# Attention over 512 heads on one core: the output tile gets ten buffers, and each store is issued later

## The chip, the cores and the metric

The kernel runs on 1 core of one Trainium2 chip. The metric is the device time of one execution in microseconds (us). Before the change the median of 4 runs is 816.46 us (815.45 to 819.59).

## The reference

```python
B, H, Sq, Sk, D = 16, 32, 192, 1024, 128
scores = jnp.einsum("bhqd,bhkd->bhqk", q, k) * scale   # scale = D ** -0.5
p = _softmax(scores, axis=-1)
return jnp.einsum("bhqk,bhkd->bhqd", p, v)
```

All tensors are bf16. For each of the 512 heads, 192 queries look at 1024 keys of width 128, and the softmax-weighted sum of 1024 values of width 128 comes out. Per head, K and V are 256 KB each, Q and the output 48 KB each.

## The kernel before

**Units.** Four heads make a quad; there are NQ = 128 quads, numbered x. A quad's scores are 8 key tiles x 192 queries = 1536 columns for each of the four heads, cut into three blocks of 512 columns, so there are NF = 384 blocks, f = 3x + b. The output work of a quad is cut into three pieces, s = 3x + i.

**The way of a quad.** SyncE (SP) loads V, K and Q of a quad (L552, L543, L530) into one of five buffers each (`f_vs`, `f_kn`, `f_qn`). VectorE (DVE) transposes K in 32x32 blocks (`turn_k`, L740) and Q (`turn_q`, L752). GpSimd (POOL) puts K into the order the matmuls want (`order`, L601) and copies V beside a column of ones (`spread`, L612); it does these in one fixed order: a block of K, the two halves of V of the quad before, two more blocks of K. TensorE (PE) makes the scores of a block (`qk`, L639), the four heads in four 32-row groups. ScalarE (ACT) takes the exponential of a block in two instructions, one head (L838) and three heads (L841). PE multiplies the exponentials with V and the ones (`pv`, L662), four blocks behind the scores (LAG = 4), so that a row's sum stands beside its result. DVE divides by the sum and writes the output tile `f_ob` (`onorm`, L761: a reciprocal, L768, and a multiplication, L772).

**What waits for what.** A load of V(x) waits until `pv` has done piece 3(x-5)+1, a load of K(x) until the K transposes of quad x-5 are done, a load of Q(x) for nothing of its own. SP's order in the loop is V(n+3), K(n+5), Q(n+5) for n = 0 to 127. PE takes a block's scores only after POOL's `order` of that block and after ACT's L838 of the block before. At the end DVE checks that all row sums lie in a safe range; a flag `redo` is then read by every engine (L21), and a second, general path is run if it is set. It isn't set with these inputs.

**The stores.** Two quads (GQ = 2) share one buffer of `f_ob` and are stored by one DMA of 384 KB; the list `stores` has 63 such pairs and two single quads of 192 KB at the end, 65 stores. Store i writes from buffer i % NSO and adds 16 to the semaphore of that buffer. DVE's first `onorm` of store i waits until store i - NSO has landed (L770). A store waits (L522) until DVE has come past its last piece. ACT issues a store behind block f = 3(x+c)+6, where x+c is the quad after the pair, that is six blocks behind the last block of the pair. 62 stores have such an f below NF. The other three (one pair, two single quads) are issued by SP at the very end of its list (L584). The function `stored` (L586) waits for all buffers' semaphores; SP runs it last.

The stores issued by ACT go through another DMA queue (q10 in the profile) than SP's loads (q1).

Of the kernel before, what the change touches and what calls it, by code (L numbers as in the profile page):

```python
# [15 lines left out]
def _only_if(nc, redo, hints):  # L16
    def wrap(body):
        def run(eng):
            name = "redo_%d" % nc.next_id()
            with eng.register() as r:  # L20
                eng.reg_load(r, redo[0:1, 0:1])  # L21
                eng.br_ne(r, 0, on_true=name + "_do", on_false=name + "_end").branch_hint(hints[eng.engine])
                with nc.body(name + "_do", valid_engines=[eng.engine]):
                    body(eng)
                    eng.br(name + "_end")
                nc.switch_bb(name + "_end")
        return run
    return wrap


def _general_path(nc, q, k, v, out, redo, hints, stored, G=16, NS=2, LAGS=(2, 4, 5, 7), ROUTES=(R_W, R_W, R_EA)):
# [16 lines left out]
    NPT = L_PV - L_EV + 2  # L48
    NSO = 2
    NRS = 4  # L50
# [6 lines left out]
    def route(u):  # L57
        return ROUTES[u % len(ROUTES)]
# [19 lines left out]
    with ExitStack() as es:  # L78
        def sb(name, shape, dt):
            return es.enter_context(nc.sbuf_tensor(name, shape, dt))  # L80
# [4 lines left out]
        def sem(name):  # L85
            return es.enter_context(nc.semaphore(name))
# [3 lines left out]
        vs = sb("vs", [128, NS, G, KT_TILES, 128], BF16)  # L90
        ob = sb("ob", [128, NSO, PPG, 4, 128], BF16)
        ss = sb("ss", [128, NSS, SK], F32)
# [13 lines left out]
        svl = [sem("svl%d" % i) for i in range(NS)]  # L106
        sst = [sem("sst%d" % i) for i in range(NSO)]
        s_qk = sem("s_qk")
# [24 lines left out]
        def store_cnt(g):  # L133
            return 48 * (g // NSO + 1)

# [12 lines left out]
        @_only_if(nc, redo, hints)  # L148
        def sync_general(e):
            stored(e)  # L150

            def loads(g):
                s = g % NS
                last_u = (g - NS + 1) * UPG - 1
                h0 = g * G
                if g >= NS:
                    e.wait_ge(s_qk, last_u + 1)
                e.dma_start_transpose(
                    kt[:, s], kf[h0:h0 + G].rearrange("g k d -> (g k) d")
                ).then_inc(sxk[s], 16)  # L160
                e.dma_start_transpose(
                    qt[:, s], qf[h0:h0 + G].rearrange("g k d -> (g k) d")
                ).then_inc(sxq[s], 16)
                if g >= NS:
                    e.wait_ge(s_pv, last_u + 1)
                e.dma_start(
                    vs[:, s], vf[h0:h0 + G].rearrange("g (p t) d -> p g t d", t=KT_TILES)
                ).then_inc(svl[s], 16)

            def stores(g):  # L170
                so = g % NSO
                e.wait_ge(s_on, (g + 1) * PPG)
                h0 = g * G
                og = of[h0:h0 + G]
                e.dma_start(
                    og[:, 0:128, :].rearrange("h p d -> p h d"),
                    ob[:, so].rearrange("p pg (x y) d -> p (pg x) (y d)", y=2)[:, :, 0:128],
                ).then_inc(sst[so], 16)
                oab = og[:, 128:192, :].rearrange("(pg x) p d -> x p pg d", x=2)
                e.dma_start(oab[0], ob[0:64, so, :, 1, :]).then_inc(sst[so], 16)  # L180
                e.dma_start(oab[1], ob[64:128, so, :, 1, :]).then_inc(sst[so], 16)

            for g in range(min(NS, NGR)):
                loads(g)
            for g in range(NGR):
                if g + NS < NGR:
                    loads(g + NS)
                stores(g)
            for so in range(min(NSO, NGR)):
                n_uses = len(range(so, NGR, NSO))  # L190
                e.wait_ge(sst[so], 48 * n_uses)

        @block.sync
        def _(e):
            sync_general(e)
            stored(e)

        @block.gpsimd
        @_only_if(nc, redo, hints)
        def _(gp):  # L200
            gp.memset(ones[:], 1.0).then_inc(s_setup, 1)
            gp.wait_ge(s_setup, 1)
            gp.affine_select(
                ident[:], ones[:], [[1, 128]], ALU.is_equal, 0.0, base=0, channel_multiplier=-1
            ).then_inc(s_setup, 1)

            def shift(u):
                gp.wait_ge(s_max, u + 1)
                if u >= NX:
                    gp.wait_ge(s_tr, u - NX + 1)  # L210
                gp.tensor_tensor(
                    x_sb[:, u % NX, :], ss[:, u % NSS, :],
                    nb[:, u % NSS: u % NSS + 1].to_broadcast([128, SK]), ALU.subtract,
                ).then_inc(s_xp, 1)

            for u in range(NU):
                if route(u) == R_W:
                    shift(u)
# [202 lines left out]
def _attention_kernel(nc, q, k, v, out):  # L421
# [9 lines left out]
    NF = 3 * NQ  # L431
# [5 lines left out]
    AHEAD = 3  # L437
    NKN, NVS, NKT, NVP = 5, 5, 2, 2
    GQ = 2
    NSO = 3  # L440
    VB = 136

    qf = q.rearrange("b h s d -> (b h) s d")
# [4 lines left out]
    stores = [(x, GQ) for x in range(0, NQ - GQ, GQ)] + [(NQ - 2, 1), (NQ - 1, 1)]  # L448
    EARLY = NF - 9

    with ExitStack() as outer:
# [28 lines left out]
        with ExitStack() as es:  # L480
# [44 lines left out]
                ).then_inc(s_st[so], 16)  # L525


            store_at = {3 * (x + c) + 6: i for i, (x, c) in enumerate(stores) if 3 * (x + c) + 6 < NF}

            def load_q(e, x):  # L530
                e.dma_start(
# [54 lines left out]
            def stored(e):  # L586
                for so in range(NSO):
                    e.wait_ge(s_st[so], 16 * len(range(so, len(stores), NSO)))
# [259 lines left out]
def bass_standalone__mha_softmax__near_ridge_kernel(  # L848
    nc: bass.Bass,
    q: bass.AP,  # L850
    k: bass.AP,
    v: bass.AP,
    out: bass.AP,
):
    _attention_kernel(nc, q, k, v, out)
# [28 lines left out]
```

## Time and profile before

| | |
|---|---|
| median of 4 runs | 816.46 us |
| the profiled execution, its own time | 818.72 us |
| its span, first to last instruction | 817.0 us |
| outside the span | 1.72 us |
| ACT L838, one of 384 | 597 ns |
| ACT L841, one of 384 | 1445 ns |
| DVE transposes of K, idle before them for the landing of K | 62.0 us of 66.3 |
| POOL copies of V, idle before them for the landing of V | 209.0 us of 213.5 |
| PE busy, by the modelled ends of its matmuls | 98% |
| granted TensorE clock, mean | 0.998 |

How to read it: the span is what the profiler saw from the first to the last instruction. An engine's busy share is a mean over the whole run, and a busy engine need not be the one that sets the pace. Idle time "before" an instruction is time in which its engine did nothing, and the profile names what ended it.

### The profile page before, as it was taken

How to read it: one execution, taken by the hardware profiler on the slowest of the kernel's cores; microseconds unless marked ns; L12 is line 12 of the kernel's file. 1: busy time of each engine (PE TensorE's matmuls, PEld its weight loads, DVE VectorE, ACT ScalarE, POOL GpSimd, SP SyncE). 2: the span in 40 equal slices, each digit the busy share in tenths (PEclk: the TensorE clock that was granted, in tenths of full speed). 3: DMA queues.
4: the chain of work that ended last, by engine and by line, in shares of the span. 5: the costliest groups of instructions: out<-in, count | busy, mean ns of one | idle time of the engine just before them, and what ended most of it. 6: DMA issues, size and time to landing. Idle time of an engine off the chain costs nothing. (4 is left out here: it accounts for less than half of the span.)

```text
span 817.0 us, 71454 instructions
## 1 busy us (share of the span) xinstructions
PE 801.9 (98%) x32996; PEld 715.0 (88%) x32996; DVE 604.3 (74%) x1293; ACT 750.0 (92%) x772; POOL 551.0 (67%) x648
## 2 busy tenths in 40 slices
PE   8999999999999999999999999999999999999997
PEld 6888888888888888888888888888888888888886
DVE  4677777777777777777777777777777777777775
ACT  6899999999999999999999999999999999999995
POOL 5667667667766766766676676676766766766674
PEclk9999999999999999999999999999999999999999
DMA  7999999999999999999999999999999999999992
GB/s 265 401 405 405 409 405 405 409 404 406 408 403 406 408 403 407 407 404 408 408 402 409 407 404 403 398 406 399 398 407 398 398 407 397 380 405 395 392 379 68
DMA packets 138454, 319.16 MB, mean 391 GB/s; under 512 B 7216, under 2 KB 56368, under 8 KB 122160
## 3 DMA queue, kind: packets, MB, share of 16 engines
q1 hardware_dynamic: 105536, 294.22, 91.9%
q10 hardware_dynamic: 32880, 24.58, 9.0%
q14 instruction: 32, 0.26, 0.1%
q8 instruction: 6, 0.10, 0.0%
HBM read 293.60 MB, written 25.17 MB: 390 GB/s over the span
## 5 line engine op out<-in xcount | busy, mean ns | idle before, releaser
L841 ACT ACTIVATE f_pt<-f_s 128x1536 bf16<-128x1536 f32 x384 | 554.9, 1445 | 0.1
L654 PE MATMUL f_s<-f_qt,f_kt 32*128 32x192 bf16 (+1 forms) x20528 | 422.7, 226 | 8.4 <-PEq L637 7.6
L683 PE MATMUL f_o<-f_vp,f_pt 128*64 128x129 bf16 x12368 | 425.9, 222 | 1.9 <-PEq L637 1.5
L683 PEld LDWEIGHTS f_o<-f_vp,f_pt 128*64 128x64 bf16 x12368 | 363.0, 110 | 51.1 <-issue 24.9
L616 POOL COPY f_vp<-f_vs 128x1024 uint32<-128x1024 uint32 x256 | 259.7, 1043 | 213.5 <-DMA f_vs<-in_v_dram 209.0
L654 PEld LDWEIGHTS f_s<-f_qt,f_kt 32*128 32x128 bf16 x20528 | 349.0, 92 | 45.6 <-issue 11.6
L747 DVE STREAM_TRANSPOSE f_kx<-f_kn 128x768 uint32<-128x768 uint32 (+1 forms) x384 | 335.1, 873 | 66.3 <-DMA f_kn<-in_k_dram 62.0
L607 POOL COPY f_kt<-f_kx 128x768 uint32<-128x768 uint32 (+1 forms) x384 | 294.6, 786 | 41.9 <-DVE f_kx L747 38.0
L838 ACT ACTIVATE f_pt<-f_s 128x512 bf16<-128x512 f32 x384 | 229.3, 597 | 58.6 <-PE f_s L654 17.9
L772 DVE TENSOR_TENSOR f_ob<-f_o,f_rinv 128x256 bf16<-128x256 f32 x381 | 161.7, 424 | 13.3 <-DVE f_rinv L768 0.3
L768 DVE RECIPROCAL f_rinv<-f_o 128x2 f32<-128x2 f32 x381 | 63.3, 166 | 128.1 <-PE f_o L683 126.2
L756 DVE STREAM_TRANSPOSE f_qt<-f_qn 128x384 uint32<-128x384 uint32 x128 | 73.0, 571 | 0.0
L825 ACT ACTIVATE f_pt<-f_ones 128x1536 f32<-128x1536 bf16 x3 | 4.2, 1472 | 0.0
L595 POOL MEMSET f_vp<- 128x1088 uint32 (+1 forms) x3 | 3.8, 1310 | 0.0
L683 PE MATMUL f_s<-f_vp,f_pt 128*64 128x129 bf16 x96 | 3.2, 220 | 0.0
L683 PEld LDWEIGHTS f_s<-f_vp,f_pt 128*64 128x64 bf16 x96 | 2.9, 110 | 0.2
L825 ACT ACT_TABLE_LOAD x1 | 1.3, 1283 | 1.2 <-PEq L869 1.2
L696 PE MATMUL f_o<-f_ones 128*128 128x512 bf16 x2 | 1.0, 620 | 1.1 <-POOL f_ones L592 1.1
L720 DVE MEMSET f_pt<- 128x256 uint32 x4 | 1.1, 272 | 0.9 <-PEq L869 0.9
L713 PE MATMUL f_o<-f_bad,f_ones 128*1 128x1 bf16 x1 | 0.2, 164 | 1.3 <-DVEq L814 1.3
L772 DVE TENSOR_TENSOR f_ob<-f_s,f_rinv 128x256 bf16<-128x256 f32 x3 | 1.3, 425 | 0.1
L768 DVE RECIPROCAL f_rinv<-f_s 128x2 f32<-128x2 f32 x3 | 0.5, 171 | 1.1 <-PE f_s L683 1.1
(15 smaller groups left out, 5.7 us busy)
## 6 DMA issues: line engine op xcount, KB each, us to landing
f_kn<-in_k_dram SPq DMA_DIRECT2D x127, 1024.0 KB, 18.1
f_vs<-in_v_dram SPq DMA_DIRECT2D x127, 1024.0 KB, 16.3
f_qn<-in_q_dram SPq DMA_DIRECT2D x127, 192.0 KB, 14.2
out_dram<-f_ob ACTq DMA_DIRECT2D x62, 384.0 KB, 9.5
f_vs<-in_v_dram SPq DMA_DIRECT2D x2, 512.0 KB, 6.5
f_kn<-in_k_dram SPq DMA_DIRECT2D x2, 512.0 KB, 4.5
out_dram<-f_ob SPq DMA_DIRECT2D x1, 384.0 KB, 3.5
out_dram<-f_ob SPq DMA_DIRECT2D x2, 192.0 KB, 2.0
```

The lines of the kernel that those rows point to most:

```text
L595: return gp.memset(part.bitcast(U32), 0x3F803F80)
L607: gp.tensor_copy(kt[:, x % NKT].bitcast(U32).rearrange("p U (j s u) c -> p U j s (u c)", s=2, u=2)[:, lo:hi], kx[:, x % 2].rearrange("p (U ...
L616: gp.tensor_copy(vp[:, x % NVP, 2 * T * i: 2 * T * i + 2 * T, 0:D].bitcast(U32), vs[:, x % NVS, 2 * i: 2 * i + 2, :].rearrange("p a (t d) ...
L654: ins = pe.matmul(S[:, c0: c0 + n1 - n0], kt[r, x % NKT, 2 * t + h, :, c], qt[r, x % R, h, n0:n1, c], start=w == 0 and g == 0, stop=w == 3 ...
L683: ins = pe.matmul(O[64 * z: 64 * z + 64, u, 0:129], pt[:, x % R, 2 * y + z, t * SQ + 64 * j: t * SQ + 64 * j + 64], vp[:, x % NVP, (2 * y ...
L747: dve.transpose(kx[:, x % 2].rearrange("p (U s j u) -> p s u U j", s=2, j=32, u=2)[:, :, :, lo:hi], kn[:, x % NKN].rearrange("p (s u U i) ...
L756: dve.transpose(qt[:, x % R].bitcast(U32).rearrange("p b (y j u) c -> p u y b (j c)", y=3, u=2), qn[:, x % NKN].rearrange("p (u y b i) -> ...
L768: dve.reciprocal(ri, O[:, :, 128]).then_inc(s_rc, 1)
L772: dve.tensor_tensor(ob[:, so, 6 * a + 2 * w: 6 * a + 2 * w + 2, :], O[:, :, 0:128], ri.unsqueeze(2).to_broadcast([128, 2, D]), ALU.mult,). ...
L825: return act.activation(part.bitcast(F32), ones[:, 0:1].to_broadcast([128, 2 * T * SQ // 2]), ACT_FN.Copy)
L838: act.activation(pt[:, x % R, 0, c], s1_ps[:], ACT_FN.Exp, scale=scale).then_inc(s_e1, 1)
L841: act.activation(pt[:, x % R, 1:4, c], s3_ps[f % 2][:], ACT_FN.Exp, scale=scale).then_inc(s_e3, 1)
```

## The change

The output tile has ten buffers in place of three (`f_ob` and its semaphores). Each store's block is 42 blocks (seven pairs of quads, HOLD = 7) later than it was, and ACT issues only the stores for which that block is at most NF - 12 = 372. That leaves 54 stores on ACT in place of 62; the first is issued behind block 54 in place of 12, the last behind block 372. The other 11 (nine pairs and the two single quads; ten pairs' worth of bytes) are issued by SP behind its last load, in the same last loop as before. A buffer is written again 20 quads later in place of 6, so the distance from a store's issue to the next write of its buffer is about eleven blocks before and after. The general path's GpSimd body also waits for all stores first; that body isn't run.

```diff
         def _(gp):
+            stored(gp)
             gp.memset(ones[:], 1.0).then_inc(s_setup, 1)
...
-    NSO = 3
+
+    NSO, HOLD = 10, 7
...
-            store_at = {3 * (x + c) + 6: i for i, (x, c) in enumerate(stores) if 3 * (x + c) + 6 < NF}
+            store_at = {3 * (x + c) + 6 + 6 * HOLD: i for i, (x, c) in enumerate(stores)
+                        if 3 * (x + c) + 6 + 6 * HOLD <= NF - 12}
```

## The prediction

> **What bounds the kernel now.** I read the page first. Three things stand near their limit: PE, ACT and the DMA.
>
> ```profile
> span 817.0 us, 71454 instructions
> ...
> PE 801.9 (98%) x32996; PEld 715.0 (88%) x32996; DVE 604.3 (74%) x1293; ACT 750.0 (92%) x772; POOL 551.0 (67%) x648
> ...
> DMA  7999999999999999999999999999999999999992
> GB/s 265 401 405 405 409 405 405 409 404 406 408 403 406 408 403 407 407 404 408 408 402 409 407 404 403 398 406 399 398 407 398 398 407 397 380 405 395 392 379 68
> ...
> q1 hardware_dynamic: 105536, 294.22, 91.9%
> q10 hardware_dynamic: 32880, 24.58, 9.0%
> q14 instruction: 32, 0.26, 0.1%
> ```
>
> The transfers are full from the second slice to the last but one, and fall from about 405 GB/s to 380-395 late. PE's ends are modelled, so its 98% doesn't decide. ACT does two instructions per block, 597 + 1445 ns. To see its pace without disturbance I took the groups of ACT in the window 60 to 110 us, then ACT's waits from 110 to 800 us.
>
> ```profile
> L838 ACT ACTIVATE f_pt<-f_s 128x512 bf16<-128x512 f32 x25 | 14.9, 597 | 2.9
> ```
>
> ```profile
> POOL f_vp L616 <- DMA f_vs<-in_v_dram: 186.4, 109, 3.0
> DVE f_rinv L768 <- PE f_o L683: 103.3, 256, 0.5
> DVE f_kx L747 <- DMA f_kn<-in_k_dram: 50.0, 89, 1.5
> POOL f_kt L607 <- DVE f_kx L747: 25.5, 84, 1.2
> PEld f_o L683 <- issue: 19.6, 116, 0.5
> ACT f_pt L838 <- PE f_s L654: 10.2, 26, 0.9
> ```
>
> In the quiet window ACT idles 2.9 / 25 = 0.116 us a block and waits for nobody: its L838 rows start 2.05 us apart there (151.05, 153.10, 155.16 in another quiet stretch), two instructions that overlap a little and that gap, and ACT sets the pace. From 110 us on it has 26 longer gaps, 10.2 us. Without the 0.116 that every block has, 10.2 - 26 x 0.116 = **7.2 us are lost to late scores**. Behind them stand POOL, which waits for V in 109 places, and DVE, which waits for K in 89. At the gap of 0.87 us before 686.3 us, POOL's copy of V at 681.99 had waited 3.03 us for its landing, the next blocks of K stood behind it on POOL, and PE idled 0.69 us before 685.12. So the kernel is ACT-paced, with a transfer stream that is just too slow for it and falls 7.2 us behind in 690 us.
>
> Are the loads late for want of bandwidth, or of free buffers? SP's own rows answer:
>
> ```profile
> 683.48 0.59 SPq L555 DMA_DIRECT2D f_vs<-in_v_dram  x1
> 684.11 1.09 SPq L546 DMA_DIRECT2D f_kn<-in_k_dram  x1
> 685.25 5.62 SPq L531 DMA_DIRECT2D f_qn<-in_q_dram  x1
> ```
>
> The Q load waits for no semaphore, and its issue still took 5.62 us: the queue was full. The waits of SP's loads that the profile puts down to PE and DVE are of this kind too: V(107) was issued at 665.0 us, and the reciprocal behind the `pv` that frees its buffer ran at 657.78. So free buffers stand idle for some 7 us before their load gets into the queue. Bandwidth is short.
>
> The tail shows how it is short. Windows of 785 to 795 and 799.6 to 802.8 us (after the times: PE, PEld, DVE, ACT, POOL, clock, DMA share, GB/s):
>
> ```profile
> 785.00:795.00 10.00, 10.00 (x430) 8.90 (x427) 8.02 (x18) 9.43 (x11) 6.26 (x9) 1.00 1.04 400
> 799.60:802.80 3.20, 2.56 (x100) 2.17 (x99) 2.64 (x5) 3.09 (x4) 2.56 (x3) 1.00 0.07 25
> ```
>
> 405 / 16 is 25.3 GB/s: at the end as much as one of sixteen DMA engines is still working, some 7 us behind the others, and the last load (V of quad 127, landed 803.2 us) waits for it. An engine that gets extra work holds up every load. Instruction fetches (q14) are such work if they go to one engine: from 110 to 800 us they are 26 packets, 0.21 MB, at 25.3 GB/s 8.3 us, about the 7.2 lost. That they all go to one engine is my inference. **The skill** against this: "Runtime: NRT & Kernel Launch", section "Instruction fetch mechanics", calls the cost of refilling mostly hidden. By that rule the 7.2 us would be ordinary shortage; the sum below is the same by either, since it takes the loss from ACT's gaps.
>
> **The change, part by part.**
>
> *Stores held for seven pairs.* From block 12 to block 54 no store runs. Seven stores fewer stand before every later load. One store takes 393,216 B / 405 GB/s = 0.97 us by bytes, or 9.0% of 817.0 / 62 = 1.19 us by its queue's share. Seven are 6.8 to 8.3 us by which each load lands earlier; I take 6.8, the end on measured bytes. Can so much be stored up? Buffers that now idle about 7 us take it, and behind them the queue is deep (16.3 us from V's issue to its landing), so no DMA engine runs dry when SP must wait for a buffer. The lead isn't spent later: seven stores stay outstanding up to the end.
>
> *What it is worth.* ACT cannot go below 2.05 us a block, so the gain is the smaller of lead and loss: min(6.8, 7.2) = **6.8 us**. The startup gaps (7.0 us of idle in 5 places before 40 us) come before any store and stay, and so does the gap of 0.82 us before 803.88, where DVE is held up by the 1.04 us check (L784) ahead of the last Q transpose. What is late next is ACT itself.
>
> *ACT's issues.* Eight fewer at 0.38 us. They are issued while L841 runs (785.10 lies before its row at 785.20, with no gap): worth 0.
>
> *DVE's wait for a buffer.* Store i is issued behind block 6i+54, its buffer is wanted near block 6i+65: eleven blocks, 22.6 us, against a landing of 9.5 us, as before. Cost 0; it would cost if a store took over 22 us.
>
> *The tail.* Eight stores fewer (54 against 62) lie before the last load, so it lands 8 x 0.97 to 8 x 1.19 us earlier, at 793.7 to 795.5, say 794.6. Behind it in SP's queue come ten pairs' worth of stores. Their price alone, without loads, is shown by the one such store of before, window 808.3 to 808.9:
>
> ```profile
> 808.30:808.90 0.60, 0.60 (x29) 0.60 (x25) 0.00 (x0) 0.60 (x2) 0.00 (x0) 1.00 0.93 293
> ```
>
> 393,216 B / 293 GB/s = 1.34 us, ten 13.4: they end near 808.0. The last store of before was issued at 813.79 behind DVE's last piece and landed 2.0 us later; 6.8 us earlier it would land at 809.0. SP looks at the landings only at 816.46 - 6.8 = 809.7 (L588, after the flag was read). So the backlog ends some 1.5 us before anyone asks for it: worth 0 to +0.4 us. SP's issues, 11 x 0.38 = 4.2 us, run beside that.
>
> *Seven more semaphore waits of SP at the end.* Four of them come after the last store's: 4 x 0.03 (the 28 ns of the L588 row) = +0.1 us. GpSimd's added wait lies in the body that isn't run: 0.
>
> Sum: -6.8 + 0.1 + 0.1 (tail, between 0 and 0.4) = -6.6 us. Against the profiled execution: span 817.0 - 6.6 = 810.4, its time 818.72 - 6.6 = 812.1. That execution lies 2.3 us over the median of the runs; the same loss from the median gives **809.9 us**.
>
> The skill has a rule against any gain: "DMA: Bandwidth & Descriptors", section "Issuing engines are not separate DMA queues", says that all queues run on the same 16 engines and another issuer only saves issue time. The bytes are indeed the same, and by that rule alone the sum would be 0. But DMA moved 0 GB/s from 803.4 to 807.0 us and isn't in the chain of waits that ends last; the order of the bytes is what the sum above prices.
>
> **The rivals.**
>
> *The tail becomes the bound (slower).* SP's queue takes the late stores one after another, and the price of one is not 1.34 but its row in the list of issues:
>
> ```profile
> out_dram<-f_ob SPq DMA_DIRECT2D x1, 384.0 KB, 3.5
> ```
>
> Then 794.6 + 10 x 3.5 = 829.6 against 815.8 for the last landing now: 13.8 us later, 830.3 us. It begins to cost above (809.7 - 794.6) / 10 = 1.5 us a store, and is slower than before above (815.8 - 794.6) / 10 = 2.1 us. Against it: loads take 16 to 18 us to land while one quad's three come every 6.2 us, so landings in one queue overlap. Chance 0.05.
>
> *The lead isn't kept (less gain).* V's buffers are the tighter ones, idle about 7 us, and 7 us of lead use all of that. If half is lost, min(3.4, 7.2) - 0.2 = 3.2 us: 813.3 us. For it: POOL's V waits are spread all over. Against it: the deep queue. Or a store in the tail costs 1.8 us, between its rows of 1.34 and 3.5, and the tail eats 10 x (1.8 - 1.5) = 3 us: about the same time. Chance 0.10.
>
> *The loads weren't the cause (no change).* The gaps are PE's own (instruction supply, since q14 packets stand near them). Then nothing moves, 816.5 us. Against it: POOL's 3.03 us wait for V at 681.99. Chance 0.05.
>
> **How the numbers follow.** Forecast 0.80, centred on 809.9; its own ends are the full loss with nothing of the tail (-7.2 - 0.7 for the last gap, 808.6) and 5 us, 811.5. The runs of before spread 1 us below their median, so the low end is 807.5. The high end takes in the half-kept lead: 813.5. A measurement of this kernel can tell about 0.5%, 4.1 us, from no change. Faster by more: the forecast and a little of the half-kept case, 0.82. Within: 0.13. Slower: 0.05.
>
> **What would show it.** ACT's gaps from 110 to 800 us should fall from 10.2 to under 2 us; DVE's waits for K from 50.0 to under 15; POOL's waits for V should shrink or be ended by PE. Loads of V in mid-run should show true waits for PE. The first GB/s slices should be as full as before, with no q10 from 38 to 124 us (42 blocks of 2.05 us later). After the last load a stretch near 290 GB/s should end before the last store's issue. If the gaps stay, the cause is wrong; if they go and the end still lies at 815, the tail is.

## The result and the profile after

The changed kernel takes 815.64 us (median of 34 runs, 811.92 to 818.65), the kernel before beside it 817.57 us (median of 55, 814.62 to 822.69). The ratio is 0.9973 with a 95% interval of [0.9962, 0.9983]: it is faster, by 2.2 us (1.4 to 3.1), and that lies within the prediction's 0.5%. Forecast were 809.9 us and a gain of 6.6. The time lies above the predicted range of 807.5 to 813.5.

The profiled execution took 814.41 us, span 812.7, against 818.72 and 817.0. From the page of the changed kernel:

```profile
span 812.7 us, 71451 instructions
...
PE 798.6 (98%) x32996; PEld 712.5 (88%) x32996; DVE 600.2 (74%) x1293; ACT 750.6 (92%) x772; POOL 553.0 (68%) x648
...
GB/s 281 400 400 402 401 400 404 409 404 405 409 405 405 408 406 405 408 405 405 408 404 405 407 406 405 404 405 403 403 395 407 388 396 395 389 406 405 387 366 167
...
q1 hardware_dynamic: 109760, 297.36, 93.8%
q10 hardware_dynamic: 28656, 21.43, 7.9%
q14 instruction: 35, 0.29, 0.1%
```

The first slices, once without stores, are as full as before: loads fill the place. q10 (ACT's stores) gave bytes to q1, where SP issues the last eleven. Its waits from 110 to 800 us (line: us in total, times, longest):

```profile
POOL f_vp L619 <- DMA f_vs<-in_v_dram: 44.8, 32, 2.2
...
DVE f_kx L750 <- DMA f_kn<-in_k_dram: 10.6, 17, 1.1
ACT f_pt L841 <- PE f_s L657: 3.2, 9, 0.8
```

Before, these three were 186.4, 50.0 and 10.2 us. The loads now come in time far more often, and ACT, which sets the pace, loses 3.2 us in 9 gaps, where it lost 10.2 in 26; beyond the 0.116 us of every block that is 1.54 us from block 11 to block 380, against 7.17 by the same count before. So the mechanism worked. The last exponential ends at 803.18 us in place of 809.93, which is 6.75 us earlier. But the span ends only 4.3 us earlier: from the last exponential to the end it is now 9.50 us, and it was 7.05. The chain of waits of the changed kernel at that point (start, duration, instruction) shows one part of the growth:

```profile
801.84 1.35 ACTq L482
803.19 0.04 issue
803.23 0.24 PE f_s L686
803.48 1.07 issue
804.55 1.97 PE f_s L686 x63
```

PE has all its inputs at 803.48 and idles for 1.07 us in the midst of its last `pv`. In the kernel before it doesn't (the same view, start, duration, instruction):

```profile
808.08 1.10 PE f_o L683 x32
809.17 3.02 PE f_s L683 x96
812.19 0.92 PE f_o L683 x32
```

The other part comes after the flag was read. The views of line 22 (the branch on `redo`) and of line 78 (behind it) have these rows of ACT, in the kernel before:

```profile
L22 ACTq COMPARE_BRANCH  x1: 68/68/68, 816.0 to 816.0; - x1
...
L78 ACTq DRAIN  x1: 85/85/85, 816.4 to 816.4; - x1
```

and in the changed kernel:

```profile
L22 ACTq COMPARE_BRANCH  x1: 68/68/68, 810.6 to 810.6; - x1
...
L78 SPq DRAIN  x1: 7/7/7, 811.3 to 811.3; - x1
...
L78 ACTq DRAIN  x1: 87/87/87, 812.4 to 812.4; - x1
```

Before, ACT needs 0.5 us from its branch to its drain (`DRAIN`, line 78). Now it needs 1.8, has nothing to compute there, and is the last engine of all: SP, which waits for all stores, was done 1.1 us before it.

So three things are to be explained: why a lead of seven stores left some gaps, why the end grew by 2 us or more, and why the ratio makes it 2.2 us where the profiled executions differ by 4.3.

### The profile page after: what moved, and what is told of

It is laid out like the page before. It is cut to its first block, busy times and chain, and to the rows that moved or that the text cites. A ratio compares the mean times of both kernels' runs of the same rounds, so it can differ in the third digit from the quotient of the medians.

```text
span 812.7 us, 71451 instructions
## 1 busy us (share of the span) xinstructions
PE 798.6 (98%) x32996; PEld 712.5 (88%) x32996; DVE 600.2 (74%) x1293; ACT 750.6 (92%) x772; POOL 553.0 (68%) x648
## 5 line engine op out<-in xcount | busy, mean ns | idle before, releaser
L610 POOL COPY f_kt<-f_kx 128x768 uint32<-128x768 uint32 (+1 forms) x384 | 301.1, 789 | 192.7 <-DVE f_kx L750 192.1
```

What stands on the lines that cost most here:

```text
L610: gp.tensor_copy(kt[:, x % NKT].bitcast(U32).rearrange("p U (j s u) c -> p U j s (u c)", s=2, u=2)[:, lo:hi], kx[:, x % 2].rearrange("p (U ...
```

## The theories

- **Lead (L)**, the prediction's: loads are late for want of bandwidth, and each store held back brings them forward. The held stores alone make the gain.
- **Its rivals for the loop**: the buffers alone do it, or the gaps are PE's or the instruction supply's, or the gain is limited by another engine.
- For the end: the **backlog (T)**, SP's late stores, disturbs PE and holds SP; or **ACT (A)**, whose list lost eight issues, comes late through the branch.
- For the rest: executions of the same kernel differ in how much the loads lose (**gaps, G**), or in something at the start or the end.

Below, "gaps" is ACT's idle time beyond 0.116 us a block from block 11 to block 380, and "end" the time from the last exponential to the end of the span. Both are summed from the rows of one profiled execution. "ACT late" means that ACT reaches its drain 1.7 us or more behind its branch.

## The experiments

**1. The changed kernel again** (no edit), for the spread between measurements.

> The changed kernel once more, for a second profile beside new times. Theory T (the tail gives it back): the last exponential ends some 6.7 us earlier than in the profile of before (803.2 against 809.9 us), and the stretch from there to the end of the span is again 1.5 to 3 us longer than the 7.1 us of before, with PE idle for about 1 us among its last multiplications and ACT late into its last block; time about 0.997 of before. Rival V (the loop varies): the tail is short in this execution, and what differs is the loop, with gaps of ACT that come and go by several us between executions; then the end of the last exponential moves by 2 us or more against 803.2 while the tail keeps its length.

Measured: 814.33 us (7 runs), ratio 0.9954 [0.9937, 0.9972]. Gaps 0.10 us, end 8.94 us, PE's idle time within the last `pv` 0.51, ACT late again.

**2. The last stores left out**, SP skips stores 55 to 61 of its eleven:

```diff
+    SKIP = range(55, 62)
...
-                    store(e, i)
+                    if i not in SKIP:
+                        store(e, i)
```

> The changed kernel without the stores 55 to 61 (the output of 14 quads is left out), so SP's late queue holds four stores instead of eleven. Theory T: with no backlog, PE's idle of 1.07 us among the last multiplications goes; the stretch from the last exponential to the end falls from 9.5 us to 8.2 or less, and the time is 1.2 us or more below the changed kernel of the same job. If ACT's late last block (1.3 us) also comes from the backlog, 2.4 us. Rival V: nothing that can be measured, within 0.5 us of the changed kernel.

Measured: 813.81 us, 0.9961 [0.9941, 0.9982]; gaps 1.57, end 9.10. With most of the backlog gone, PE still stops in its last `pv`, and ACT is still late (timeline of PE, then line 78):

```profile
804.36 1.97 PE L688 MATMUL f_s<-f_vp,f_pt 128*64 128x129 bf16 x63 [0.51 <-issue]
```

```profile
L78 ACTq DRAIN  x1: 87/87/87, 812.3 to 812.3; - x1
```

T falls as the cause of either: the backlog isn't on the path. PE's idle time of 0.51 us is that of experiment 1, which had the whole backlog. The fall of 1.2 us in time that T expected did not come.

**3. Ten buffers alone**, stores issued where they were: `NSO, HOLD = 10, 0`, all 62 on ACT.

> Ten buffers alone, each store issued where it was before (HOLD = 0, 62 stores on ACT). Every theory: no change, within 0.1% of before, ACT's gaps from 110 to 800 us about 10 us, since a buffer's wait was never the bound. If it is faster by 0.2% or more, the room in the buffers and not the order of the stores made the gain.

Measured: 817.51 us, 0.9999 [0.9983, 1.0016]. Gaps 7.41 us, ACT's wait as before:

```profile
ACT f_pt L841 <- PE f_s L657: 10.9, 30, 0.7
```

The buffers are only the room for the lead and give nothing by themselves.

**4. More instruction bytes in the kernel before**: sixteen increments of an unread semaphore per quad in SP's loop, which make SP's program 131,072 bytes longer (39,424 to 170,496).

```diff
+                    for _ in range(16):
+                        e.sem_inc(s_pad, 1)
```

> The kernel before with 16 more instructions of SP per quad that only add to a semaphore nobody waits for: 131,072 bytes more of SP's program to fetch, and no other work. Theory F (instruction fetches run on one DMA engine and hold up every load there): 16 more fetch packets of 8 KB, at 25.3 GB/s 5.2 us more on that engine; ACT's gaps rise from 10 to about 15 us and the time by 4 to 5 us. Rival (fetches are hidden, the shortage is one of bandwidth over all engines): 0.13 MB more of 319 MB is 0.04%, 0.3 us; no change that can be measured.

Measured: 829.45 us, 1.0144 [1.0121, 1.0168], +11.8 us; gaps 15.40 us. The DMA view of 110 to 800 us, first the kernel before, then the padded one:

```profile
q14 instruction: 26, 0.21, 0.1%
```

```profile
q14 instruction: 40, 0.33, 0.1%
```

Fourteen more packets, +8.2 us of gaps: 0.59 us a packet, where a packet takes 8,192 B / 25.3 GB/s = 0.32 us on one engine by itself (an estimate from the forecast's rate of one engine). Of the 10.4 us between the two spans 8.2 are these gaps, 1.4 a later start of block 11 and 0.6 the end. The increments also take about 1.0 us of SP's own time in each quad. SP still has time for them, since its loads mostly stand before a full queue (timeline of SP in the padded kernel):

```profile
300.66 0.38 SPq L556 DMA_DIRECT2D f_vs<-in_v_dram  x1
301.09 4.33 SPq L547 DMA_DIRECT2D f_kn<-in_k_dram  x1
305.46 0.65 SPq L532 DMA_DIRECT2D f_qn<-in_q_dram  x1
```

Spread over all sixteen engines at 405 GB/s the 114,688 bytes would cost 0.28 us. So a longer program of an engine that isn't busy sets back the loads by far more than its bytes. That the fetches do it, and not SP's 1.0 us a quad, is argued: an edit that takes the time without the bytes wasn't run. That one DMA engine takes all the fetches fits, and isn't shown: the packets' engine isn't among the rows read here, and nearly twice the price of one engine stays unexplained.

**5. ACT's list as long as before**: the changed kernel with eight increments of an unread semaphore behind the blocks where ACT's first stores were.

```diff
+                    if f in range(12, 60, 6) and f not in store_at:
+                        act.sem_inc(s_pad, 1)
+                    if f == 54:
+                        act.sem_inc(s_pad, 1)
```

> The changed kernel with eight instructions put back into ACT's list, one for each store that left it: each adds 1 to a semaphore that nobody waits for, behind blocks 12 to 54. ACT's program has its old length again (218,880 bytes in place of 218,368). Theory A (the late end of ACT is a fetch of its last code, which the 512 bytes moved over a boundary): ACT comes into its last block 0.5 us after its branch, not 1.8; the end lies 2.3 us behind the flag's write in place of 3.6, and the time is 1.3 us below the changed kernel of this job. Rival B (the late stores hold up that fetch): 3.6 us stay, no change.

Measured: 813.72 us, 0.9962 [0.9947, 0.9978]. The late ACT is gone:

```profile
L22 ACTq COMPARE_BRANCH  x1: 68/68/68, 812.0 to 812.0; - x1
...
L78 ACTq DRAIN  x1: 85/85/85, 812.5 to 812.5; - x1
```

Branch to drain is 0.5 us again, and from the write of the flag to the end it is 2.45 us in place of 3.59. The 1.3 us expected in the time did not show: it isn't told apart from the changed kernel's 813.84 beside it (experiment 8). This profile has gaps of 2.56 us.

**6. Four pairs held**: `NSO, HOLD = 7, 4`.

> Hold of four pairs and seven buffers. Theory L (the gain is the lead, some 0.85 us per held store): lead 3.4 us in place of 6.0; ACT's gaps in the loop 4 to 5 us (before 7.2, with seven 0.1 to 1.6), the last exponential 2.5 us later than with seven, time between before and the changed kernel, 1 to 2 us above the latter. Rival V (what the runs show is chance between executions): no order between four and seven.

Measured: 814.73 us, 0.9969 [0.9956, 0.9982]. The gaps expected are absent: 0.10 us.

```profile
ACT f_pt L841 <- PE f_s L657: 1.1, 2, 0.9
```

A likely reason is that block 11 of this execution starts at 37.80 us, 2.7 us later than in the changed kernel's first profile, and a loop that begins later needs its loads later by as much: at quads 21 to 36 a load of V enters the queue 0.98 us after its buffer came free, about as soon as with seven pairs (0.5 to 2.0 us in seven profiles). So four and seven pairs aren't told apart here, in the ratio either (0.9956 [0.9941, 0.9972] for seven, experiment 8). With eight late stores in SP's list its ACT isn't late (drain 0.48 us behind the branch), which again speaks against the backlog and for something in ACT's own program.

**7. Nine pairs held**: `NSO, HOLD = 12, 9`.

> Hold of nine pairs and twelve buffers. Theory L with V's buffers as the cap (V's issue stood only 0.4 to 1.2 us behind its buffer's release at 120 us): the lead grows by 1 us at most, loop gaps 0 to 1 us; two more late stores in the tail cost up to 2 us there. Time within 1 us of the changed kernel. Rival (lead without a cap, no cost in the tail): 1.5 us faster than seven.

Measured: 813.66 us, 0.9948 [0.9933, 0.9963]. No gaps (0.00); POOL hardly waits for V any more, 2.4 us against the changed kernel's 44.8:

```profile
POOL f_vp L619 <- DMA f_vs<-in_v_dram: 2.4, 5, 0.8
...
ACT f_pt L841 <- PE f_s L657: 1.0, 1, 1.0
```

The end is 9.04 us, with ACT late.

**8. The changed kernel a third time** (no edit), beside 5 to 7.

> The changed kernel a third time, as the measure for the other three of this job. Loop gaps 0.1 to 1.6 us, from the flag's write to the end 3.6 us, time 0.995 to 0.998 of before.

Measured: 813.84 us, 0.9956 [0.9941, 0.9972]; gaps 0.18, end 9.46.

**9. A later start of the loop, in the kernel before.** Two activations of 1.45 us on ACT behind blocks 9 and 10, into a tile that nobody reads:

```diff
+                    if f in (9, 10):
+                        act.activation(idle[:, f - 9, :], ones[:, 0:1].to_broadcast([128, 1536]), ACT_FN.Copy)
```

> The kernel before with two more ACT instructions of 1.45 us, behind blocks 9 and 10, that write a tile nobody reads: the exponentials start 2.9 us later for good. Theory S (before, the transfers set the end, and a late start is made up by fewer gaps): ACT's gaps from block 11 to 380 fall from 7.2 to about 5 us, and the time rises by 1 us or less. Rival (ACT's work and the gaps simply add up): gaps stay at 7 us, time +2.9 us.

Measured: 818.33 us, 1.0002 [0.9988, 1.0016]. ACT does 2.9 us more work, block 11 starts 3.0 us later, and the time is the same, because the gaps fall from 7.17 to 3.80 us (counted without the step before block 11, which the added work fills, here and in experiment 10):

```profile
ACT f_pt L839 <- PE f_s L655: 5.0, 11, 0.9
```

That is the plainest evidence that before the change the transfers set the end of the loop and not ACT.

**10. The same edit in the changed kernel.**

> The same two instructions in the changed kernel. Theory S (after, ACT sets the end from the first block on, so what the start costs goes through in full): gaps 0 to 1 us as without them, last exponential 2.5 to 2.9 us later than the changed kernel's, time +2 to +3 us on it, so most of the gain on before is gone. That would also explain why the changed kernel's gain differs between executions, whose first blocks end up to 3 us apart. Rival: time +1 us or less, as before.

Measured: 813.94 us, 0.9960 [0.9946, 0.9975]. The cost expected did not come. Block 11 starts 2.5 us later than in the changed kernel's first profile, gaps are 0.10 us, and the last exponential ends at 803.59 us, as in the others:

```profile
ACT f_pt L842 <- PE f_s L658: 0.6, 2, 0.4
```

ACT isn't late here (0.48 us), which by itself saves some 1.2 us at the end, so the time alone doesn't say that the extra work was free. So the changed kernel still stands at the edge between ACT and transfers: its lead is about as large as its loss, and a later start is still partly paid for by gaps that vanish.

**11. Nine pairs held and ACT's list lengthened** by ten increments:

```diff
-    NSO, HOLD = 10, 7
+    NSO, HOLD = 12, 9
...
+                    elif f in range(6, 66, 6):
+                        act.sem_inc(s_pad, 1)
```

> The best of what was seen, meant to beat both: hold of nine pairs, twelve buffers, and ten instructions put back into ACT's list so that its program is 218,880 bytes as before. Loop gaps 0 (nine pairs), end 2.4 us behind the flag's write (old length): 1.3 us faster than nine pairs alone, ratio to before about 0.993. If the length of ACT's program was not the cause of its late end, 0.995.

Measured: 811.89 us (7 runs, 811.11 to 817.47), 0.9941 [0.9918, 0.9963], the lowest median of all. No gaps, end 8.40, ACT not late:

```profile
ACT f_pt L842 <- PE f_s L658: 0.6, 1, 0.6
```

```profile
L22 ACTq COMPARE_BRANCH  x1: 68/68/68, 808.9 to 808.9; - x1
...
L78 ACTq DRAIN  x1: 85/85/85, 809.3 to 809.3; - x1
```

It beats the kernel before by 4.8 us (3.0 to 6.7). The changed kernel was timed beside it (experiment 12, 815.49 us in 12 runs): six of the seven runs here, 811.11 to 812.82, are below the lowest there, 813.07.

**12. The changed kernel a fourth time** (no edit), beside 9 to 11.

> The changed kernel as the measure for this job: gaps from block 9 on 0.1 to 1.6 us, the last exponential 770.8 us plus those gaps behind the exponential of block 9, ratio 0.995 to 0.998.

Measured: 815.49 us, 0.9974 [0.9962, 0.9987]; gaps 2.58, end 9.43.

**13. The changed kernel three times more and experiment 11 once more** (no edits), a single profiled execution each.

> The changed kernel, one more execution with its profile (one of four), to catch one of the slow ones: between executions it takes 811.9 to 818.7 us. Theory G (in a slow execution the transfers are slower and the lead runs out earlier): over 816 us, ACT's gaps from 110 to 800 us are 5 us or more, with starts and tails like the others'. Theory H (the start or the tail differs): gaps stay under 3 us, and the exponential of block 11 ends 2 us or more later than 36 us, or the tail is over 11 us.

> As the look before it: G expects the time to follow the gaps of the loop one for one (814 us with gaps near 1.5, 818 us with 5 or more), H the start or the tail.

> As the two looks before it: G expects the time to follow the gaps of the loop, H the start or the tail.

> Nine pairs with ACT's old program length, one more look beside them on the same chip. Theory G: with more lead no gaps or under 1.5 us, time 810 to 813 us. Theory H: it varies as the changed kernel does.

Measured: 813.50, 817.24, 812.48 and 813.66 us. The slowest and the fastest of the changed kernel's show how much of a difference between executions is gaps. ACT and POOL in the slow one, 110 to 800 us:

```profile
POOL f_vp L619 <- DMA f_vs<-in_v_dram: 52.5, 35, 2.2
...
ACT f_pt L841 <- PE f_s L657: 5.4, 15, 1.0
```

and in the fast one:

```profile
POOL f_vp L619 <- DMA f_vs<-in_v_dram: 16.8, 14, 1.8
...
ACT f_pt L841 <- PE f_s L657: 1.3, 2, 1.1
```

Of the 4.75 us between them, 2.75 are gaps (2.85 against 0.10), 1.2 the start of block 11 and 0.9 the end. G holds for the greater part, not for all. Neither mark set beforehand decides it: the slow execution has 5.4 us of gaps by the view, over G's 5, but 2.85 by the count of the table, under H's 3. Nine pairs had no gaps in three profiles out of three (experiments 7, 11 and its repetition).

All of it in one table (us; the changed kernel has seven profiles, "before and alike" are before and experiments 3 and 9):

| | last exponential ends | gaps | end | branch to drain of ACT |
|---|---|---|---|---|
| before and alike | 809.5 to 809.9 | 3.8 to 7.4 | 7.0 to 7.8 | 0.5 |
| changed kernel, mean | 803.3 | 1.1 (0.1 to 2.9) | 9.4 (8.9 to 9.9) | 1.7 to 2.2 |
| late stores left out (2) | 803.6 | 1.6 | 9.1 | 2.0 |
| ACT padded (5) | 804.9 | 2.6 | 8.3 | 0.5 |
| four pairs (6) | 804.4 | 0.1 | 7.7 | 0.5 |
| nine pairs (7) | 803.5 | 0.0 | 9.0 | 1.8 |
| nine pairs, padded (11; two profiles) | 801.8, 803.4 | 0.0 | 8.4, 8.6 | 0.5 |

The last column goes with the length of ACT's program as built: 218,240 and 218,368 bytes (nine pairs, changed kernel, experiment 2) are late, 218,496 to 219,008 bytes (experiments 10, 6, before, 3, 5, 11, 9) are not. Eight issues fewer take 512 bytes. That it is ACT's program and nothing else of the change is shown by experiment 5, which restores the length and nothing more, and by 11 against 7. The packets of queue q14 (instructions, 8 KB each) say how: in all nine profiles with a late ACT one starts 0.17 to 0.28 us after ACT's branch, and in the nine others none does within 1.05 us of it. So a late ACT, by these times, waits for instructions to be fetched. Why a shorter program makes that fetch necessary isn't shown.

PE's stop in its last `pv` goes with an instruction packet too, of queue q8 (16 KB each). From 797 to 803 us the DMA view of the changed kernel has one:

```profile
q8 instruction: 1, 0.02, 1.0%
```

The stop is always at one place of PE's program, between the first and the second matmul of output piece 381. The step between these two takes 0.20 to 1.58 us, its neighbours mostly 0.03, and in all eighteen profiles the second one starts 1.24 to 1.49 us after such a packet has ended. In the changed kernel's first profile the packet ends at 803.18 us and the matmul starts at 804.55; in the kernel before the packet ends at 808.90 and the matmul starts at 810.22, after a step of only 0.23. So PE, by these times, waits there for its own code, and the later the packet comes the longer it stands. No experiment moved that packet, and what makes it come earlier or later is open.

## Why the prediction was wrong, point by point

**Right.** *Bandwidth is short* and the held stores cure it: ten buffers alone 0.9999, four, seven and nine pairs each faster. *What it is worth*, 6.8 us, is what the loop gained: the last exponential ends 6.5 us earlier (803.3 as a mean of seven profiles against 809.8 of before and experiment 3). The lead per store was taken as 0.97 us; after seven stores the time from a V buffer's release to its load's entry into the queue fell from 7.55 to 1.20 us (quads 21 to 36), 0.91 us a store (0.52 to 2.02 us in the other six profiles). It isn't kept by standing still, as the text had it: by quads 101 to 116 that time is 7.27 us again, so the lead is spent against the loss along the way, which is what it is for. Of the marks named, DVE's waits for K (10.6, under 15), the full first slices and the true waits of V's loads for PE came as said; ACT's gaps in that view fell to 3.2 us, not under 2. The backlog ended before the last store's issue: V of the last quad landed at 796.0 us (taken 794.6), and SP's nine stores of pairs landed from 797.02 to 805.43 us, 1.05 us apart, where 1.34 was taken. SP's issues of these stores took longer than the 0.38 us each of the text (1.12 us in the median), at no cost.

**Wrong: "*ACT's issues.* Eight fewer at 0.38 us … worth 0".** They were priced as time on ACT, and the length of ACT's program was put at nothing without a reason. It costs 1.2 to 1.3 us at the end, with ACT the last engine. Experiment 5 removes it (3.59 to 2.45 us from the flag to the end).

**Wrong: "worth 0 to +0.4 us" for the tail.** The end grew by 2.0 us (9.4 as a mean of seven profiles against 7.4 of before and experiment 3): ACT's 1.3, and 0.65 of PE's idle time in the last `pv` (0.91 against 0.26 in the same means). The backlog cost nothing, as the sum had it, and was the wrong suspect: experiment 2 took most of it away and both stayed. PE's stop goes with the packet of its code, as said above. It appears in every kernel that holds stores, also where ACT isn't late, and in two that hold none (0.51 us in experiment 3, 0.54 in experiment 4); so that holding the stores makes it longer is seen in the profiles and not explained.

**Wrong: "min(6.8, 7.2)" from one execution.** The loss differs from execution to execution, some 4 to 9 us in the changed kernel, as an estimate from the gaps that remained and from how far the time before V's entry grew again (in the fastest profile of the changed kernel to 5.1 us by quads 101 to 116, in the slowest to 7.5); with 6.3 us of lead (7.55 - 1.20) some executions have no gaps and others 2.9 us. The gain is a mean of minima, smaller than the minimum of two means: 1.1 us of gaps remain on average. Nine pairs cover the loss in all three profiles.

**Wrong: the level.** The forecast stood on a median of four runs, 816.46; of 55 runs it is 817.57. That is 1.1 of the 5.7 us of the miss.

The sum: the loop 0.3 less and the end 1.8 more than forecast, 2.1 of the profiles' 2.3 us (814.4 in the mean against 812.1 forecast); 1.1 from the level. The remaining 2.3 us come from carrying a gain read off profiles to the medians. Profiles differ by 818.72 - 814.4 = 4.3 us, the medians of the first measurement by 1.9. Part of that is chance: four measurements of the same kernel gave 0.9973, 0.9954, 0.9956 and 0.9974, a gain of 2.1 to 3.8 us. Part is that the profiled executions of before and of experiment 3 lay 1.2 and 1.7 us above their medians, so that a loss read from them is too large; that of experiment 9 lay on its median, so this is argued and not shown.

The rule of the Trainium skill that was weighed, "DMA: Bandwidth & Descriptors", section "Issuing engines are not separate DMA queues", says that the queues share the same 16 engines and that another issuer saves only issue time; taken alone it gave no gain at all. The measured ratio of 0.9973 [0.9962, 0.9983], and 0.9948 [0.9933, 0.9963] with nine pairs, adds that the order of the same bytes matters where something else can wait. The other, "Runtime: NRT & Kernel Launch", section "Instruction fetch mechanics", calls refilling mostly hidden; here 131,072 bytes more of an engine that isn't busy came with 11.8 us more.

## What to carry to other kernels

Where the transfers are just too slow for the engine that sets the pace, deferring traffic that nobody waits for behind the last needed load is a real gain; give it more lead than the loss of one profiled execution shows, since the loss varies. A test for which side sets the end is to add work to the pacing engine at the start: if the time stays (1.0002 with 2.9 us more), the transfers do. And look at the end of the run when an engine's list gets shorter or longer: a microsecond may stand there that has nothing to do with the change's purpose. Instruction packets near the place where an engine stands still are worth a look.

## What the runs showed of the hardware that was not expected

- Eight issues (512 bytes) fewer in ACT's program made its way from the last branch to its drain 1.7 to 2.2 us long in place of 0.5, with an 8 KB instruction packet 0.17 to 0.28 us behind the branch; padding restored it.
- PE stopped for 0.5 to 1.3 us in the midst of its last multiplications, with all inputs there, and went on 1.24 to 1.49 us after a 16 KB instruction packet had ended.
- 131,072 bytes more in the program of SP, with fourteen more instruction packets of 8 KB beside full transfers, came with 8.2 us more of ACT's gaps (0.59 us a packet), and 11.8 us more in all (1.0144 [1.0121, 1.0168]).
- Stores of 384 KB that stand behind each other in one queue landed 1.05 us apart; the single one of before took 3.5 us from issue to landing.
- 2.9 us more work on the engine that seems to set the pace cost nothing before the change (1.0002 [0.9988, 1.0016]). After it the last exponential ended at 803.59 us, against 803.3 as the mean of seven profiles without the extra work.
